# Turning one of six groups of probability blocks by a DMA transpose, in an attention and mixture-of-experts kernel on one NeuronCore

## The chip, the core and the metric

The kernel runs on one NeuronCore of a Trainium2 chip (trn2). The core has TensorE (PE in the profile; PEld are its weight loads), VectorE (DVE), ScalarE (ACT), GpSimd (POOL) and SyncE (SP, which here only issues DMAs). Every engine works through its own queue in order, and the engines wait for each other by semaphores. The metric is the time of one execution on the device, in microseconds (us); the median of several runs counts.

## The reference

The program computes block-causal attention over 8 batches of 8 heads, with 576 positions of 64 features, and then sends every position through one of 8 experts.

```python
scores = scale * np.matmul(q, k.transpose(0, 1, 3, 2))        # q, k, v: (8, 8, 576, 64)
mask = block_i >= block_j                                     # blocks of 64 positions
scores = np.where(mask, scores, -1000000000.0)
attn = softmax(scores); attn_out = np.matmul(attn, v)
x = attn_out.transpose(0, 2, 1, 3).reshape(B * S, H * D)      # 4608 x 512
expert_idx = np.argmax(x @ w_gate, axis=1)                    # one of 8, gate_w its probability
out[mask_e] = gate_w * (relu(x @ w1[e]) @ w2[e])              # w1: 512 x 1024, w2: 1024 x 512
```

All tensors are fp32.

## The kernel before, in words

The attention part works on 32 pairs of heads (four pairs to a batch). For one pair the queries are cut into four row blocks of 128 (`i` = 1 to 4) and a first block of 64; the two heads of the pair are `j` = 0 and 1, "A" and "B" in the names of the steps. The steps of a pair, with the lines that the profile shows:

- `ld` (L106 to L108) issues three DMAs on SP: keys `kd`, queries `qd`, values `v`, about 1 MB together. `cK`, `cQ` (ACT) and `lK`, `lQ` (DVE) split keys and queries into a high and a low part, so that scores come out of three products.
- `S1` to `S4`, `S0` (PE, L203 and L191) are the scores. The two heads run side by side on 64 rows of the array each. `K` (DVE memsets, L215) hides masked blocks, `M` (DVE, L220) takes the negative maximum of a row, `E` (ACT, L235) the exponential with its row sums. They write the probabilities `pb`, one fp32 tile of 128 partitions for a pair.
- The probabilities must be turned before they meet the values. That is done in six groups of four 128x128 blocks, `k0`, `a1`, `b1`, `a2`, `b2`, `x3`, and a small one, `t0`. `T` (PE, L274) transposes a group into a PSUM tile `pt` (two buffers), `H` (L286) copies it to an SBUF tile `ph` on the engine behind the `@` of its name.
- `V0` to `V5` (PE, L305) are the products with the values, the two heads on 64 columns of the array each. `V1` reads `a1` and `b1`, `V2` and `V4` read `a2` and `b2`, `V3` reads `x3`, `V0` reads `k0`, `V5` reads `t0`. `O`, `O0` copy the product out of PSUM.
- `F` (PE, L340 and L334) turns it back and multiplies by the gate's weights, `X`, `Y` (DVE) scale it. `R1`, `R2` (DVE) invert the sums, `Z` and `q0` (POOL) scale the small first block.

The order of all steps is written out by hand in the string `ORDER`. An entry `Tb1:3` means: in turn number t do step `Tb1` for pair t - 3. A turn goes through the whole string once, so each engine's queue gets its steps in that order, and four or five pairs are in work at a time. `z0` to `z6` are places for the router's small steps (one batch's after its fourth pair), `y0`, `y1` for pieces of POOL's work: scatters of the router's table and the splitting of the first expert's weights. When a batch is done, its rows go to memory by DMAs on SP (`xd`), about 1.1 MB.

The expert part follows when the last pair is done. It has a DMA transpose of its own, on ACT's queue (L996): ACT writes the two 16-bit halves of fp32 numbers as separate planes (L984), the DMA turns them, ACT joins them (L1002). The change does not touch that part.

Of the kernel before, what the change touches and what calls it, by code (L numbers as in the profile page):

```python
# [8 lines left out]
F32 = mybir.dt.float32  # L9
F32R = mybir.dt.float32r  # L10
BF16 = mybir.dt.bfloat16
U16 = mybir.dt.uint16
# [6 lines left out]
P = 128  # L19
# [11 lines left out]
POFF = (None, 0, 384, 1024, 1920)  # L31
PCOLS = 3072
# [7 lines left out]
class Attention:  # L40
# [8 lines left out]
    def __init__(self, ctx, tc, ident, qT, kT, vt, w_gate, ends, po):  # L49
# [8 lines left out]
        self.raw = ctx.enter_context(tc.tile_pool(name="araw", bufs=3))  # L58
        self.rawk = ctx.enter_context(tc.tile_pool(name="arawk", bufs=2))
        self.rawv = ctx.enter_context(tc.tile_pool(name="arawv", bufs=5))  # L60
        self.spl = ctx.enter_context(tc.tile_pool(name="aspl", bufs=2))
        self.pt = ctx.enter_context(tc.tile_pool(name="apt", bufs=9))
        self.sm = ctx.enter_context(tc.tile_pool(name="asm", bufs=3))
# [8 lines left out]
        self.bank, self.ptile, self.ph, self.oT, self.xs = {}, {}, {}, {}, {}  # L72
        self.small_bank, self.at = (None, None), {}
# [176 lines left out]
    def op_T(self, m, x):  # L250

# [5 lines left out]
        pb = self.pb[m]  # L260
        todo = {
# [6 lines left out]
        }.get(x)  # L268
# [4 lines left out]
        for n, o in enumerate(todo):  # L273
            self.nc.tensor.transpose(t[:, P * n : P * n + P], pb[:, o : o + P], self.ident)  # L274

    def copy(self, engine):
        return self.nc.scalar.copy if engine == "A" else self.nc.vector.tensor_copy
# [86 lines left out]
    def step(self, name, m):  # L364
# [9 lines left out]
        elif k == "T":  # L374
            self.op_T(m, name[1:])
# [19 lines left out]
    def run(self, order, sink, part, other, then, loaded):  # L395
# [9 lines left out]
        first = dict(order)["E1B"]  # L405
# [5 lines left out]
        for turn in range(self.M + last):  # L411
            if turn == first and dict(order)["S0"] < first:

                turns = [x for x in order if x[0] not in ("M0", "E0")]
                n = turns.index(("E1B", turn)) + 1
                turns[n:n] = [(x, turn) for x in ("S0", "M0", "E0")]
            else:
                turns = [x for x in order if x[0] != "S0" or turn > x[1] or x[1] == first]
            if turn == self.M + last - 1:
                turns = [(x, lag) for name, lag in order for x in ends.get(name, (name,))]  # L420
            for name, lag in turns:
# [11 lines left out]
                if not 0 <= m < self.M or (name == "ld" and m < 2):  # L433
                    continue
                self.step(name, m)
                if name == "ld":
                    loaded(m)
# [22 lines left out]
M1A:3 ld:0 V1:4 V3:4 V4:4 M1B:3 M3B:3 E1A:3 E1B:3 V5:4 Ta1:3 S0:3 lQ:2 E3B:3 z5:0 M0:3 z3:0 S4:2 O@A:4 Tk0:3 O0@D:4  # L460
z6:0 Ha1@A:3 Tb2:3 K4B:2 E0:3 q0:2 Hk0@A:3 F1:4 K4A:2 Hb2@A:3 M4B:2 M4A:2 X1:4 Tb1:3 E4B:2 y0:0 Y1:4 z4:0 z1:0 E4A:2
# [930 lines left out]
```

## Time and profile before

| | before |
|---|---|
| median of 3 runs | 830.76 us (830.45 to 830.93) |
| the profiled execution | 832.52 us |
| its span, from the first to the last instruction | 830.8 us |
| mean granted TensorE clock | 0.992 of full speed |
| PE, PEld, DVE, ACT, POOL busy | 808.1, 634.0, 420.8, 554.8, 357.0 us |
| HBM read, written | 76.76 MB, 21.98 MB |

A row of the profile names the line of the kernel, the engine, the operation and its tiles (out<-in, buffer numbers sometimes kept: `pt2b` is group b of pair 2), their shapes, and the time. Matmuls overlap each other, so the time from one start to the next says what one costs. The span is shorter than the execution's own time, 832.52 us, which holds what lies around the first and the last instruction.

### The profile page before, as it was taken

The numbers are of one execution on the slowest core, as the hardware profiler recorded it, in microseconds if no ns is written. First come the engines' busy times: TensorE is split into PE (matmuls) and PEld (weight loads), VectorE is DVE, ScalarE is ACT, GpSimd is POOL, SyncE is SP. The second block draws the span as 40 slices with busy tenths as digits, with TensorE's granted clock in tenths as the row PEclk, the third lists the DMA queues.
The fourth block names the chain that finished last, engine by engine and source line by source line (L and its number), as shares of the span: only waits on it lengthen the run. The fifth ranks groups of instructions, "written<-read, shape, count | busy, mean of one in ns | idle before, by whom it ended". The sixth has DMA issues, their size and how long they took to land.

```text
span 830.8 us, 16466 instructions
## 1 busy us (share of the span) xinstructions
PE 808.1 (97%) x5126; PEld 634.0 (76%) x5126; DVE 420.8 (51%) x1208; ACT 554.8 (67%) x1254; POOL 357.0 (43%) x392
## 2 busy tenths in 40 slices
PE   5999999999999999989899999999999999999996
PEld 4777777777777777768788888888888888888884
DVE  5677788888878878657604400046646444000000
ACT  6999899889898889724454555455546554554552
POOL 3000133333322502263745654466656655544553
PEclk8999999999999999999999999999999999999999
DMA  6335757464545537335826513346766853133212
GB/s 206 99 104 153 152 139 169 123 159 123 148 121 140 126 111 185 83 71 161 266 77 164 178 51 77 77 137 169 240 182 175 265 152 75 42 76 77 67 48 67
DMA packets 83706, 108.80 MB, mean 131 GB/s; under 512 B 45601, under 2 KB 48929, under 8 KB 83618
## 3 DMA queue, kind: packets, MB, share of 16 engines
q1 hardware_dynamic: 38082, 78.26, 33.1%
q0 software_dynamic: 7520, 19.97, 8.3%
q10 hardware_dynamic: 38016, 9.44, 6.8%
q8 instruction: 50, 0.82, 0.4%
q14 instruction: 38, 0.31, 0.1%
HBM read 76.76 MB, written 21.98 MB: 119 GB/s over the span
## 4 chain that ended last, share of the span: by engine, by line
PE 87%; issue 3%; POOL 2%; ACT 2%; DMA 1%; DVE 1%; POOLq 1%; DVEq 0%; SPq 0%; ACTq 0%
PE py L1058 23%; PE o L305 12%; PE ph L937 12%; PE o L937 12%; PE ya L203 6%; PE xa L203 3%; PE o L340 3%; PE px L896 2%; PE pt L1019 2%; PE o L334 1%; ACT pb L235 1%; POOL tab L732 1%; PE o L191 1%; DMA out<-y,idx 0%; PE o L1359 0%
## 5 line engine op out<-in xcount | busy, mean ns | idle before, releaser
L1058 PE MATMUL py<-w,low 128*128 (+1 forms) x912 | 226.9, 398 | 0.8 <-ACT low L1010 0.8
L1058 PEld LDWEIGHTS py<-w,low 128*128 128x128 f32 x912 | 168.8, 188 | 38.1 <-issue 1.2
L1181 DVE CAST w<-raw 128x1024 fp32r<-128x1024 f32 x60 | 49.3, 866 | 182.1 <-PE o L937 131.5
L248 POOL TENSOR_SCALAR p<-p,rs 128x64 f32<-128x64 f32 x32 | 14.2, 445 | 249.7 <-DVE rs L244 166.8
L1038 POOL TENSOR_TENSOR low<-h,low 128x512 fp32r<-128x512 f32 x72 | 105.2, 1464 | 24.7 <-ACT h L1011 24.7
L915 POOL TENSOR_TENSOR xl<-xf,xh 128x512 fp32r<-128x512 f32 x38 | 50.7, 1335 | 109.0 <-ACT xf L909 108.8
L1187 DVE TENSOR_TENSOR w<-raw,w 128x1024 fp32r<-128x1024 f32 x60 | 83.9, 1455 | 0.0
L906 ACT CAST xh<-px 128x512 fp32r<-128x512 f32 x38 | 22.3, 588 | 90.7 <-PE px L896 89.0
L937 PE MATMUL ph<-w,xh 128*128 x280 | 76.3, 395 | 0.0
L937 PE MATMUL o<-w,xh 128*128 x280 | 75.8, 393 | 0.0
L984 ACT COPY h<-ph 128x1024 uint16<-128x1024 uint16 x36 | 36.5, 1012 | 47.2 <-PE ph L937 26.0
L975 ACT ACTIVATE h<-o 128x512 f32<-128x512 f32 x37 | 22.2, 600 | 62.5 <-PE o L937 48.1
L937 PEld LDWEIGHTS ph<-w,xh 128*128 128x128 f32 x280 | 53.2, 190 | 12.1
L937 PEld LDWEIGHTS o<-w,xh 128*128 128x128 f32 x280 | 52.6, 188 | 11.7
L1082 POOL DMA_INDIRECT out<-y,idx x35 | 39.8, 1138 | 41.0 <-issue 37.0
L235 ACT ACTIVATE pb<-ya,neg 128x320 f32<-128x320 f32 (+2 forms) x93 | 48.6, 532 | 2.3 <-PE pt30x L274 1.6
L878 POOL DMA_INDIRECT xg<-xd,idx x37 | 45.3, 1226 | 10.2 <-POOL idx L874 9.2
L235 ACT ACTIVATE pb<-yb,neg 128x320 f32<-128x320 f32 (+2 forms) x93 | 49.4, 546 | 0.0
L732 POOL DMA_INDIRECT tab<-toks,posi x40 | 41.7, 1044 | 15.0 <-issue 14.2
L1002 ACT COPY h<-hf 128x1024 uint16<-128x1024 uint16 x36 | 43.3, 1203 | 5.1 <-DMA hf<-h 5.1
L220 DVE TENSOR_REDUCE neg<-ya 128x1 f32<-128x320 f32 (+2 forms) x93 | 44.8, 481 | 0.0
L220 DVE TENSOR_REDUCE neg<-yb 128x1 f32<-128x320 f32 (+2 forms) x93 | 41.9, 478 | 3.3 <-ACT pb L235 1.3
(966 smaller groups left out, 2132.3 us busy)
## 6 DMA issues: line engine op xcount, KB each, us to landing
raw<-w SPq DMA_DIRECT2D x60, 512.0 KB
qd<-qT SPq DMA_DIRECT2D x32, 352.0 KB
v<-vt SPq DMA_DIRECT2D x32, 352.0 KB
kd<-kT SPq DMA_DIRECT2D x32, 288.0 KB
xd<-xt SPq DMA_DIRECT2D x7, 1026.0 KB
xd<-xg SPq DMA_DIRECT2D x9, 256.5 KB
xg<-w SPq DMA_DIRECT2D x8, 256.0 KB
xd<-x SPq DMA_DIRECT2D x8, 128.0 KB
```

Of the source, the lines that this page charges most:

```text
L203: ins = mm(out, q[x][r, 128 * (i - 1) : 128 * i], q[y][r, o : o + w], start=n == 0, stop=n == 2, skip_group_check=True,)
L220: ins = self.nc.vector.tensor_reduce(self.neg[m][:, c : c + 1], src, AX.XY if i == 4 else AX.X, ALU.max, negate=True)
L235: ins = self.nc.scalar.activation(dst, src, AF.Exp, bias=self.neg[m][:, c : c + 1], scale=1.0, accum_out=self.sums[m][:, c : c + 1])
L305: self.nc.tensor.matmul(out[r], self.raws[m][2][:, slot], self.ph[m, bank][:, c0:c1], start=t in (0, 5), stop=t in (4, 5), skip_group_chec ...
L732: put = self.nc.gpsimd.indirect_dma_start(out=self.tab[:, :], out_offset=bass.IndirectOffsetOnAxis(ap=posi[:, i : i + 1], axis=0), in_=sel ...
L878: pool.indirect_dma_start(out=self.xg[i], out_offset=None, in_=self.xd[:, :], in_offset=bass.IndirectOffsetOnAxis(ap=self.idx[:, t : t + 1 ...
L915: pool.tensor_sub(self.xl, self.xf, self.xh).then_inc(sem["xp"], 1)
L937: m = pe.matmul(self.ph[f], x[:, P * k : P * k + P], weights(k, f, part), start=start and k == 0, stop=stop and k == 3,)
L1038: engine.tensor_sub(hl, self.hf if t < 2 else self.h[f], hh).then_inc(sem["hp"], 1)
L1058: m = pe.matmul(self.py[t % 2], h[:, c // 4, P * (c % 4) : P * (c % 4) + P], wf[:, bass.ds(off + (base + 512 * c), 512)], start=n == 0, st ...
L1181: dve.tensor_copy(hi, raw[m % nr]).then_inc(sem["wh"], 1)
L1187: dve.tensor_sub(lo, raw[m % nr], hi).then_inc(sem["wd"], 1)
```

## The change

The group `b1` is no longer transposed by PE. Three new steps take its place. `Db1` copies the four blocks to a tile of 16-bit numbers, first the low halves of all fp32 numbers, then the high halves (two buffers, which are halves of a weight buffer that is not yet in use, `raw[4]`). `Ib1` issues a DMA transpose of that tile on SP's queue. `Jb1` joins the two turned planes to fp32 numbers in a `ph` tile. The engines stand behind the `@` in the new order: `Db1@A` is on ACT, `Jb1@P` on POOL. For `Db1` to read the four blocks with one step, the places of the row blocks in `pb` move (`POFF`, and the tile grows from 3072 to 3840 columns).

The order of all steps is new. Two copies move from ACT to DVE (`Hb2`, `O`). `V1` and `V3` now come a turn later than `V0`, `V2`, `V4` and `V5` of the same pair. `qd` has four buffers instead of three, `kd` three instead of two, and the special places of `S0`, `M0`, `E0` in the first turns are worked out anew.

```diff
--- before.py
+++ after.py
@@ -28,8 +28,8 @@
 HIDE = -(2.0**100)
 
 
-POFF = (None, 0, 384, 1024, 1920)
-PCOLS = 3072
+POFF = (None, 0, 896, 1792, 2688)
+PCOLS = 3840
 VS = 11
 
 QS = 512 + P + D
@@ -46,7 +46,7 @@
 
 
 
-    def __init__(self, ctx, tc, ident, qT, kT, vt, w_gate, ends, po):
+    def __init__(self, ctx, tc, ident, qT, kT, vt, w_gate, ends, po, spare):
         self.tc, self.nc = tc, tc.nc
         self.qT, self.kT, self.vt = qT, kT, vt
         self.po = po
@@ -55,11 +55,12 @@
         self.M = qT.shape[0] * H // 2
         nc = self.nc
         cp = ctx.enter_context(tc.tile_pool(name="acst", bufs=1))
-        self.raw = ctx.enter_context(tc.tile_pool(name="araw", bufs=3))
-        self.rawk = ctx.enter_context(tc.tile_pool(name="arawk", bufs=2))
+        self.raw = ctx.enter_context(tc.tile_pool(name="araw", bufs=4))
+        self.rawk = ctx.enter_context(tc.tile_pool(name="arawk", bufs=3))
         self.rawv = ctx.enter_context(tc.tile_pool(name="arawv", bufs=5))
         self.spl = ctx.enter_context(tc.tile_pool(name="aspl", bufs=2))
         self.pt = ctx.enter_context(tc.tile_pool(name="apt", bufs=9))
+        self.pl = ctx.enter_context(tc.tile_pool(name="apl", bufs=2))
         self.sm = ctx.enter_context(tc.tile_pool(name="asm", bufs=3))
         self.ot = ctx.enter_context(tc.tile_pool(name="aot", bufs=2))
         self.xp = ctx.enter_context(tc.tile_pool(name="axp", bufs=2))
@@ -70,6 +71,8 @@
         self.raws, self.qs = {}, {}
         self.pb, self.sums, self.neg, self.rs = {}, {}, {}, {}
         self.bank, self.ptile, self.ph, self.oT, self.xs = {}, {}, {}, {}, {}
+        self.planes, self.turned = {}, {}
+        self.pl0 = [spare[:, 512 * i : 512 * i + 512].bitcast(U16) for i in range(2)]
         self.small_bank, self.at = (None, None), {}
         self.used = {}
         self.op_ld(0)
@@ -247,34 +250,56 @@
         t = self.p0[m]
         self.nc.gpsimd.tensor_scalar(t, t, self.rs[m][:, 8:9], None, ALU.mult)
 
-    def op_T(self, m, x):
-
-
-
-
+    def blocks(self, x):
 
         def at(j, i, t):
 
             return POFF[i] + (P * i + P * t if j else P * (i - t))
 
-        pb = self.pb[m]
-        todo = {
+        return {
             "k0": [POFF[i] + P * i for i in range(1, 5)],
             "a1": [at(0, i, 1) for i in range(1, 5)],
             "b1": [at(1, i, 1) for i in range(1, 5)],
             "a2": [at(0, 2, 2), at(0, 3, 2), at(0, 4, 2), at(0, 4, 4)],
             "b2": [at(1, 2, 2), at(1, 3, 2), at(1, 4, 2), at(1, 4, 4)],
             "x3": [at(0, 3, 3), at(0, 4, 3), at(1, 3, 3), at(1, 4, 3)],
-        }.get(x)
+        }[x]
+
+    def op_T(self, m, x):
+
         t = self.ptile[m, x] = self.ps_t.tile([P, 512], F32, tag="pt", name=f"pt{m}{x}")
         if x == "t0":
             self.nc.tensor.transpose(t[0:64, 0:P], self.p0[m], self.ident)
             return
-        for n, o in enumerate(todo):
-            self.nc.tensor.transpose(t[:, P * n : P * n + P], pb[:, o : o + P], self.ident)
+        for n, o in enumerate(self.blocks(x)):
+            self.nc.tensor.transpose(t[:, P * n : P * n + P], self.pb[m][:, o : o + P], self.ident)
+
+    def op_D(self, m, x, engine):
+
+        o = self.blocks(x)
+        assert all(b - a == o[1] - o[0] for a, b in zip(o, o[1:]))
+        step = 2 * (o[1] - o[0])
+        t = self.planes[m, x] = self.pl0[m % 2]
+        src = self.pb[m].bitcast(U16)[:, 2 * o[0] : 2 * o[0] + 3 * step + 256]
+        pad = self.pb[m].bitcast(U16)[:, 2 * o[0] : 2 * o[0] + 1]
+        src = bass.AP(pad.tensor, pad.offset, [list(pad.ap[0]), [1, 2], [step, 4], [2, P]])
+        self.copy(engine)(t.rearrange("p (o n c) -> p o n c", o=2, n=4), src)
+
+    def op_I(self, m, x):
+
+        t = self.turned[m, x] = self.pl.tile([P, 1024], U16, tag="tt", name=f"tt{m}{x}")
+        self.nc.sync.dma_start_transpose(t.rearrange("p (k c) -> p k c", c=P), self.planes.pop((m, x)))
+
+    def op_J(self, m, x, engine):
+
+        h = self.ph[m, x] = self.pt.tile([P, 512], F32, tag="ph", name=f"ph{m}{x}")
+        self.copy(engine)(
+            h.bitcast(U16).rearrange("p (c o) -> p o c", o=2),
+            self.turned.pop((m, x)).rearrange("p (o c) -> p o c", o=2),
+        )
 
     def copy(self, engine):
-        return self.nc.scalar.copy if engine == "A" else self.nc.vector.tensor_copy
+        return {"A": self.nc.scalar.copy, "D": self.nc.vector.tensor_copy, "P": self.nc.gpsimd.tensor_copy}[engine]
 
     def op_H(self, m, x, engine):
         t = self.ptile.pop((m, x))
@@ -371,8 +396,10 @@
             getattr(self, "op_" + name)(m, engine)
         elif k == "H":
             self.op_H(m, name[1:], engine)
-        elif k == "T":
-            self.op_T(m, name[1:])
+        elif k in "TI":
+            getattr(self, "op_" + k)(m, name[1:])
+        elif k in "DJ":
+            getattr(self, "op_" + k)(m, name[1:], engine)
         elif k == "Y":
             self.op_Y(m, int(name[1]), engine)
         elif k in "KME":
@@ -402,20 +429,16 @@
         last = max(lag for name, lag in order if name[0] not in "yz")
         left = [20] * (self.M // 4)
         more, pace, asks = iter(()), 1, None
-        first = dict(order)["E1B"]
+        at = {name: (lag, n) for n, (name, lag) in enumerate(order)}
+        after = max(("E1B", "E2B"), key=at.get)
+        late = ("S0", "M0", "E0") if at["S0"] < at[after] else ()
 
         ends = {
             "F1": ("F2", "F0"), "X1": ("X2", "Y0@D"), "Y1": ("Y2",), "F2": ("F1",), "X2": ("X1",), "Y2": ("Y1",),
             "F0": (), "Y0@D": (),
         }
         for turn in range(self.M + last):
-            if turn == first and dict(order)["S0"] < first:
-
-                turns = [x for x in order if x[0] not in ("M0", "E0")]
-                n = turns.index(("E1B", turn)) + 1
-                turns[n:n] = [(x, turn) for x in ("S0", "M0", "E0")]
-            else:
-                turns = [x for x in order if x[0] != "S0" or turn > x[1] or x[1] == first]
+            turns = order
             if turn == self.M + last - 1:
                 turns = [(x, lag) for name, lag in order for x in ends.get(name, (name,))]
             for name, lag in turns:
@@ -432,7 +455,12 @@
                     next(then)
                 if not 0 <= m < self.M or (name == "ld" and m < 2):
                     continue
+                if m == 0 and name in late:
+                    continue
                 self.step(name, m)
+                if m == 0 and name == after:
+                    for x in late:
+                        self.step(x, 0)
                 if name == "ld":
                     loaded(m)
                 if name == "F1" and asks == "bank":
@@ -457,10 +485,10 @@
 
 
 ORDER = """
-M1A:3 ld:0 V1:4 V3:4 V4:4 M1B:3 M3B:3 E1A:3 E1B:3 V5:4 Ta1:3 S0:3 lQ:2 E3B:3 z5:0 M0:3 z3:0 S4:2 O@A:4 Tk0:3 O0@D:4
-z6:0 Ha1@A:3 Tb2:3 K4B:2 E0:3 q0:2 Hk0@A:3 F1:4 K4A:2 Hb2@A:3 M4B:2 M4A:2 X1:4 Tb1:3 E4B:2 y0:0 Y1:4 z4:0 z1:0 E4A:2
-Ta2:3 z0:0 F0:4 F2:4 Hb1@A:3 cQ:1 S2:2 Ha2@A:3 R1:3 S1:2 lK:1 R2:3 X2:4 Y0@D:4 K1A:2 K2A:2 K2B:2 S3:2 M2A:2 Z:3 K1B:2
-K3A:2 Tx3:3 M2B:2 y1:0 cK:0 E2A:2 Hx3@A:3 M3A:2 K3B:2 Tt0:3 E2B:2 E3A:2 Ht0@D:3 z2:0 V0:3 V2:3 Y2:4
+Hx3@A:4 cK:1 Db1@A:3 y0:0 S4:2 V1:4 M0:3 Hb2@D:3 z4:0 Ib1:3 V3:4 Tk0:3 K4A:2 K4B:2 Ta1:3 M4A:2 E0:3 M4B:2 O@D:4 ld:0
+z3:0 E4A:2 E4B:2 F1:4 R1:3 lK:1 Y1:4 S1:2 S2:2 z1:0 z6:0 R2:3 X1:4 Hk0@A:3 S3:2 Ha1@A:3 F0:4 cQ:1 K1B:2 F2:4 z5:0
+M1B:2 Z:3 Ta2:3 q0:2 E1B:2 Ha2@A:3 K3B:2 K1A:2 M3B:2 Tt0:3 V0:3 K2A:2 K2B:2 V2:3 M2A:2 M1A:2 M2B:2 X2:4 z2:0 V4:3
+Y0@D:4 Y2:4 E3B:2 E2A:2 Ht0@D:3 V5:3 Jb1@P:3 Tx3:3 S0:2 K3A:2 M3A:2 E2B:2 lQ:1 E1A:2 Tb2:2 E3A:2 z0:0 O0@D:3 y1:0
 """
 
 
@@ -1286,7 +1314,7 @@
     po = ctx.enter_context(tc.tile_pool(name="pso", bufs=1, space=PSUM))
 
     with ExitStack() as actx:
-        att = Attention(actx, tc, ident, qT, kT, vt, w_gate, y, po)
+        att = Attention(actx, tc, ident, qT, kT, vt, w_gate, y, po, raw[4])
         router = Router(rcst, tp, sp, tc, B, xd, tab, ident)
 
         def weights(n):
```

## Rows read from the trace of the kernel before

**Rows 1.** The page: span, busy times, and the busy tenths of the span's 40 slices (20.8 us each) for DVE; PEclk is the granted TensorE clock in tenths of full speed.
```profile
span 830.8 us, 16466 instructions
...
PE 808.1 (97%) x5126; PEld 634.0 (76%) x5126; DVE 420.8 (51%) x1208; ACT 554.8 (67%) x1254; POOL 357.0 (43%) x392
...
DVE  5677788888878878657604400046646444000000
...
PEclk8999999999999999999999999999999999999999
```

**Rows 2.** Busy time by stretches of the attention part: from and to (us), length, busy us of PE, PEld, DVE, ACT and POOL with the number of instructions, granted clock, DMA share, GB/s. The first is a turn without the router's steps, the second the fullest of four turns in a row with them (203.10 to 245.80 us), the third the sum and the means of those four.
```profile
31.90:42.50 10.60, 10.60 (x95) 7.84 (x95) 7.87 (x29) 9.57 (x28) 0.94 (x3) 1.00 0.31 97
...
235.00:245.80 10.80, 10.71 (x95) 7.88 (x95) 9.23 (x35) 9.82 (x29) 2.87 (x5) 1.00 0.30 100
sum 42.70, PE 42.61 PEld 31.49 DVE 34.38 ACT 38.44 POOL 12.88; mean PE 10.65 PEld 7.87 DVE 8.60 ACT 9.61 POOL 3.22
```

**Rows 3.** Waits between 100 and 300 us, all engines: who waited for whom, us in total, times, longest.
```profile
DVE neg L220 <- PE o L191: 14.5, 18, 1.0
DVE xb L215 <- PE xb L203: 9.6, 14, 0.8
```

**Rows 4.** One turn of PE (pair 2 in most steps) in order of time: start us, us, what. L274 are the transposes `T`, L203 the scores `S`, L191 `S0`, L340 `F1` and `F2`, L271 `Tt0`, L305 the products `V`.
```profile
37.68 0.33 PE L191 MATMUL o<-qd,q 128*128 128x64 f32 x2
37.95 0.40 PE L203 MATMUL xa<-kh,qh 64*128 64x288 f32 x1
...
38.18 0.29 PE L203 MATMUL xa<-kl,qh 64*128 64x288 f32 x1
...
38.72 0.29 PE L203 MATMUL xa<-kh,ql 64*128 64x288 f32 x1
...
38.94 0.66 PE L274 MATMUL pt2k<-ident,pb 128*128 128x128 f32 x4
39.44 0.60 PE L274 MATMUL pt2b<-ident,pb 128*128 128x128 f32 x4
39.87 0.66 PE L340 MATMUL o<-fold,oT 128*128 128x144 f32 x4
40.37 0.60 PE L274 MATMUL pt2b<-ident,pb 128*128 128x128 f32 x4
40.80 0.62 PE L274 MATMUL pt2a<-ident,pb 128*128 128x128 f32 x4
...
44.30 0.27 PE L271 MATMUL pt2t<-ident,p 128*64 128x128 f32 x1
44.50 1.08 PE L305 MATMUL o<-ph2k,v 128*64 128x512 f32 x4
45.41 0.49 PE L305 MATMUL o<-ph2a,v 128*64 128x384 f32 x1
...
46.06 0.59 PE L305 MATMUL o<-ph2a,v 128*64 128x512 f32 x1
...
46.91 0.60 PE L305 MATMUL o<-ph2x,v 128*64 128x256 f32 x4
```

**Rows 5.** ACT: two steps of the same turn in order of time (a copy `H` and the exponential behind it), then the lines of the experts' own DMA transpose (planes, issue, join: count, duration min/median/max in ns) and the time from its issue to its landing.
```profile
40.12 0.59 ACT L286 COPY ph2b<-pt2b 128x512 f32<-128x512 f32 x1
40.60 0.76 ACT L235 ACTIVATE pb<-xb,neg 128x576 f32<-128x576 f32 x1
...
L984 ACT COPY h<-ph x36: 1012/1012/1016, 384.5 to 808.3; 128x1024 uint16<-128x1024 uint16 x36
L996 ACTq DMA_TRANSPOSE hf<-h x36: 1248/1252/2350, 386.8 to 809.4; - x36
L1002 ACT COPY h<-hf x36: 1163/1207/1212, 395.0 to 816.2; 128x1024 uint16<-128x1024 uint16 x36
...
DMA to landing us min/median/max: 3.9/4.1/8.1
```

**Rows 6.** DVE's copies from PSUM: count, duration min/median/max in ns, first and last start.
```profile
L316 DVE COPY o<-o x32: 211/214/241, 27.6 to 356.6; 128x64 f32<-128x64 f32 x32
L356 DVE COPY x<-o x32: 286/290/291, 32.1 to 358.5; 64x144 f32<-64x144 f32 x32
```

**Rows 7.** POOL's steps with one input (L248, L132) and with two (L1308), in the same form, and DVE's `lQ` (L123), whose longest is the one that starts at 282.47.
```profile
L248 POOL TENSOR_SCALAR p<-p,rs x32: 442/445/447, 19.9 to 352.5; 128x64 f32<-128x64 f32 x32
L132 POOL TENSOR_SCALAR q<-qd x32: 522/532/978, 5.4 to 334.1; 128x128 f32<-128x128 f32 x32
L1308 POOL TENSOR_TENSOR high<-xg,zero x8: 1266/1276/1290, 119.7 to 282.1; 128x512 fp32r<-128x512 f32 x8
L123 DVE SCALAR_TENSOR_TENSOR ql<-qd,qh x32: 671/681/1402, 5.3 to 336.6; 128x512 fp32r<-128x512 f32 x32
...
282.47 1.40 DVE L123 SCALAR_TENSOR_TENSOR ql<-qd,qh 128x512 fp32r<-128x512 f32 x1
```

**Rows 8.** ACT at the end of the attention part, in order of time: the last pair's last exponential and its row sum, and the copy of its product.
```profile
347.91 0.66 ACT L235 ACTIVATE pb<-yb,neg 128x448 f32<-128x448 f32 x1
348.43 0.24 ACT L235 ACTIVATION_READ_ACCUMULATOR pb<-yb,neg 128x1 f32 x1
...
356.47 0.59 ACT L312 COPY oT<-o 128x512 f32<-128x512 f32 x1 [2.70 <-PE o L305]
```

**Rows 9.** Busy time by stretches again, columns as in rows 2: ten microseconds in which a batch's rows are written.
```profile
222.00:232.00 10.00, 10.00 (x88) 7.26 (x88) 7.66 (x34) 9.17 (x27) 3.07 (x4) 1.00 0.99 201
```

## The prediction

> **What bounds the kernel now.** I read the page first, then a table of busy time by stretches, the waits, and one turn instruction by instruction. The page [rows 1] shows TensorE (PE) busy 97% of the span; the VectorE (DVE) digits end their dense part near the 18th of 40 slices of 20.8 us, which is where the 32 pairs of heads end (about 356 us); behind it come the experts, which the change does not touch. The granted clock there is full speed, 2.4 GHz, but for one early slice, so no term below is a clock term. The table [rows 2] is the view that decides: in a turn (one step of every kind, each for its own pair) PE is busy all of 10.60 us, ScalarE (ACT) 9.57, DVE 7.87, GpSimd (POOL) 0.94. Over four turns with the router's steps among them the means are 10.65 for PE, 9.61, 8.60 and 3.22, and the fullest turn has 9.23 of DVE. So PE sets the pace, ACT is 90% full, and DVE has some 2 us of slack a turn, partly spent waiting for PE itself, 14.5 and 9.6 us in 200 us on two lines [rows 3].
>
> A busy PE need not be at its peak, so the turn itself has to be read [rows 4]. Four 128x128 transposes cost 0.43 us where they follow their own kind (pt2b at 39.44 to 39.87, and 40.37 to 40.80). PE runs three tile shapes: 64-row scores (`64*128`), 64-column value products (`128*64`), and the full array. Where the shape changes, time is lost: the last scores at 38.72 to Tk0 at 38.94 is 0.22 against 0.135 inside the block (38.18 to 38.72 in four steps), and Tk0 then takes 0.50, not 0.43: together 0.15. From Tt0 (44.30) to V0 (44.50) is 0.20 against 0.11, and V0 takes 0.91 against 0.85 for the equal V1 (46.06 to 46.91): 0.15. S0 at 37.68 to the first scores and on to the second (37.95, 38.18) loses 0.25. The old order has six such changes a turn.
>
> **The change, part by part.** *Removed from PE:* Tb1, four transposes, 0.43 to 0.44 us a pair [rows 4]. That lies wholly on the engine that sets the pace.
>
> *Added to PE:* the new order puts V1 and V3 behind S4, apart from V0, V2, V4, V5. Counting along the order string, the shapes go scores, value, full, scores, full, value, full: seven changes where six stood. The new kind, scores to value, is not in the trace; it lies between 0 and the largest seen, 0.25, and I take 0.15, which both kinds nearest to it cost [rows 4]. The Trainium skill, TensorEngine Tiling (Array Packing), section Key Properties, says that changing the tiling mode drains the engine; the gaps at the changes of shape agree with it. By it the split has a price and the sum below stands at -3.9 us; without it the sum would be -8.6 (31 times 0.15 better). So PE's turn changes by -0.44 + 0.15 = -0.29 us, bounds -0.44 and -0.19.
>
> *ACT:* it loses three 128x512 copies (Hb1 goes, Hb2 and O move to DVE), 0.48 each from start to start (40.12 to 40.60, [rows 5]), and gains the planes Db1. The diff's order line has `Db1@A`: ACT makes the planes, and only the join is POOL's. The nearest rows are the experts' splits of as many 16-bit elements, 1.01 and 1.21 us [rows 5]; I take 1.1. Net -0.34: ACT goes to about 9.25 of 10.4 and does not set the pace.
>
> *DVE:* Hb2 and O, two copies of 128x512 from PSUM. DVE copies of 64 and 144 columns take 0.214 and 0.290 [rows 6]: 0.95 ns a column, so 0.64 for 512, about 0.6 from start to start; lower bound 0.5 (what ACT needs), upper 0.65. DVE gains 1.2 a turn: 9.8 mean, 10.43 in the fullest turn. Against PE turns of 10.36 mean and 10.51 for that fullest one, the slack that hid DVE's waits falls from 2.05 to 0.56 us. And the order leans on DVE: V5 on PE needs Ht0, which stands behind ten memsets and reductions, X2, Y0 and Y2 on DVE; F1 needs O, behind the four steps K4 and M4. DVE must wait for PE at least twice a turn, some 0.2 us each (scores to memset). So the fullest turn wants 10.43 + 0.4 = 10.83, 0.32 over PE; the others fit. That is 0.08 a turn on average; I take 0.10, bounds 0 and 0.5.
>
> *POOL:* the join Jb1, 1024 elements. Its one-input rows give 445 ns for 64 columns and 532 for 128 [rows 7]: 1.36 ns each, so 1.75 us; a two-input row, 1.28 for 512, gives 1.86 ns each, so 2.25. POOL rises from 3.2 to 5 us a turn and stays slack. Behind Jb1 on POOL stand one or two router or weight pieces, then q0 and Z half a turn later; S0 and Tt0 wait for those. A join late by under 3 us delays neither.
>
> *The transpose.* Ib1 stands on SP's queue before the next pair's loads and waits for Db1; behind it wait the loads, the batch's writes and the first expert's pieces. The loads are used a turn later, and they no longer wait for buffers (four and three instead of three and two), so an Ib1 in time costs them nothing. Landing took 4.1 us median, 3.9 to 8.1 [rows 5]. The chain, from the end of Tx3: Hx3, cK, Db1 on ACT 0.5 + 0.6 + 1.1 = 2.2 (cK has 576 columns, so a little over the copy's 0.48), up to 0.7 more for the exponential E3A that stands before Hx3 (one of its width took 0.66, [rows 8]), landing 4.1, join 1.75, semaphores 0.2: 8.9 us. V1 of that pair comes a turn and S0, Tb2, S4 later on PE (0.27 + 0.44 + 0.99, rows 4), at 12.1. So the whole chain is hidden, with 3.2 us to spare. After each batch SP's queue is full for 10 us (DMA share 0.99 from 222 to 232, [rows 9]); the writes are issued behind Ib1 of their turn, so the next Ib1 meets at most the last microsecond or two. I take 0.
>
> *Ends.* Startup has the same lags: 0, within 1 us. At the end nothing hides the chain. Before, the last exponential ends at 348.67 and the copy of the finished product starts at 356.47: 7.8 us [rows 8]. After: Hx3 0.5, planes 1.1, landing 4.1, join 1.75, V1 0.85 and V3 0.43 (half the columns), changes and semaphores 0.8: 9.6. I take +2 us, bounds 1 and 6 (landing 8.1).
>
> *Sum.* A turn: -0.44 + 0.15 + 0.10 = -0.19; 31 turns lie between the first pair and the last, so -5.9; ends +2.0; together -3.9 us. The profiled execution took 832.52 (span 830.8), so 828.6 for its like; it lies 1.8 above the median 830.76, for which I say 826.9.
>
> **Rivals.** *All hidden:* no price for the seventh change of shape, no wait for DVE: 31 times -0.44, ends +1.5, is -12 us, 818.6. For it: PE hardly waited before [rows 3]. Against it: the gaps at changes of shape.
>
> *DVE sets the pace (the other side):* place V5 behind Ht0, price DVE's total plus its waits. If 0.9 of the former 2.05 us of idle time stays, a turn is 9.8 + 0.9 = 10.7, 0.05 over the old mean; 31 turns and the ends give +3.6, 834.3. It decides from 0.23 us of PE waiting a turn, where the gain is gone. For it: the 10.43 of the fullest turn. Against it: the new order fills the two long waits of [rows 3] with the moved copies.
>
> *The join is late:* if landings under the pairs' loads are like the slowest row, 8.1, the chain needs 12.9 and V1 waits 0.8 us. In every second turn with a join at the upper bound (1.3 us) that is 16 times 1.3 = +21, with the other terms 844. For it: the loads share SP's queue; against it: the median 4.1 was taken under weight loads too.
>
> *POOL holds DVE up:* at 282.47 DVE's `ql` took 1402 ns instead of 681, under two POOL instructions [rows 7]. If the join met such a DVE step every turn, DVE would have 9.8 + 0.72 + 0.4 = 10.9 against PE's 10.36, 0.46 more than the forecast's 10.46: 31 times 0.46 is +14, 841. The join falls by my placing between lK and lQ, so only a late one meets them. The Trainium skill, SBUF — State Buffer, calls the port pair that both engines use an exclusive lock which blocks the loser for the whole instruction, for DVE steps with two SBUF inputs; the doubled row agrees.
>
> **Chances.** Forecast 0.42 (822 to 830), all hidden 0.20 (817 to 822), DVE 0.20 (831 to 837), late join 0.10 (837 and more), lock 0.08 (834 to 845). The range 818 to 838 leaves out the far ends of the first and the last two, about 0.17; the forecast's own is 822 to 830. This measurement tells some 0.2%, 1.7 us, from no change: faster (under 829.1) 0.58, same 0.12, slower 0.30.
>
> **What would show it.** PE's turn without router steps at 10.25 to 10.4 (10.60 now); a gap of 0.05 to 0.1 between S4 and V1; DVE 9 to 9.8 us in a turn; V5 with short waits on the copy of Ht0, none at V1; landings of 4 to 5 us; the join at 1.7 to 2.3. Long waits before V1, or joins that start late, prove the sum wrong; so does a DVE that never idles beside a PE that does.

## The result: 0.9% slower, and the profile after

The changed kernel took 838.64 us (median of 3 runs, 837.36 to 838.91) where the kernel before took 830.76: a ratio of 1.0091, 95% interval 1.0068 to 1.0114. The forecast was 826.9 with a range to 838, so it was wrong in sign and just outside its range. The page after, in the rows that answer to [rows 1]:

```profile
span 836.4 us, 16259 instructions
...
PE 807.2 (97%) x4998; PEld 615.6 (74%) x4998; DVE 465.9 (56%) x1272; ACT 539.1 (64%) x1190; POOL 397.7 (48%) x424
```

PE is still 97% busy: its sum says nothing of what happened. The table by stretches, as in [rows 2], does: a turn without router steps, then the turns of pairs 10, 14 and 18.

```profile
41.05:51.58 10.53, 10.48 (x91) 7.27 (x91) 9.13 (x31) 9.06 (x27) 2.22 (x3) 1.00 0.41 121
104.70:118.33 13.63, 12.57 (x103) 8.32 (x101) 10.91 (x40) 9.34 (x27) 4.97 (x8) 1.00 1.11 168
151.50:164.10 12.60, 12.56 (x103) 8.32 (x101) 10.93 (x40) 9.34 (x27) 4.97 (x8) 1.00 1.00 163
196.30:208.96 12.66, 11.93 (x104) 8.16 (x100) 11.74 (x39) 9.35 (x28) 5.04 (x8) 1.00 0.77 155
```

The turn without router steps went from 10.58 to 10.53, and once in every four turns stands one of 11.75 to 13.6 us, where before none exceeded 11.4. DVE is 10.9 to 11.7 us busy in those. From the rounding of q of pair 2 to that of pair 31 it is 319.6 us (310.9 before). The last copy oT of the attention part starts 9.2 us later; the experts' start then takes 3.6 us less, so that 5.6 remain in the span. The waits from 100 to 300 us, as in [rows 3]:

```profile
PEld o L330 <- DVE h L308: 7.6, 6, 1.6
PE o L330 <- DVE h L308: 6.2, 5, 1.3
PE o L330 <- POOL ph8b L296: 1.0, 1, 1.0
POOL ph8b L296 <- DMA tt8b<-raw: 6.5, 1, 6.5
POOL ph12b L296 <- DMA tt12b<-raw: 5.5, 1, 5.5
```

Two new waits: V5 for the copy Ht0 (6.2 us of PE; the 7.6 us of its weight loads, PEld, are the same waits seen a second time), and the join for transposes issued behind a batch's writes, with V1 behind it. These landed late: tt8b 10.1 us after issue, where the next one took 3.6.

```profile
tt8b<-raw SPq DMA_TRANSPOSE x1, 10.1
tt9b<-raw SPq DMA_TRANSPOSE x1, 3.6
```

V1 has two halves, one for each head, which start together in other turns. For pair 8 the half that reads b1 starts 2.09 us after the half that reads a1, as soon as the join ends:

```profile
111.65 1.07 PE L330 MATMUL o<-ph8a,v 128*64 128x512 f32 x2
113.74 0.64 PE L330 MATMUL o<-ph8b,v 128*64 128x512 f32 x1 [1.02 <-POOL ph8b L296]
```

### The profile page after: what moved, and what is told of

Its sections match the earlier page's. It is cut to its first block, busy times and chain, and to the rows that moved or that the text cites. A ratio compares the mean times of both kernels' runs of the same rounds, so it can differ in the third digit from the quotient of the medians.

```text
span 836.4 us, 16259 instructions
## 1 busy us (share of the span) xinstructions
PE 807.2 (97%) x4998; PEld 615.6 (74%) x4998; DVE 465.9 (56%) x1272; ACT 539.1 (64%) x1190; POOL 397.7 (48%) x424
## 4 chain that ended last, share of the span: by engine, by line
PE 80%; DVE 9%; ACT 3%; DMA 3%; issue 2%; POOL 2%; POOLq 0%; SPq 0%; DVEq 0%; ACTq 0%
PE py L1086 24%; PE ph L965 12%; PE o L965 12%; PE o L330 7%; DVE neg L223 4%; PE ya L206 4%; PE o L365 4%; PE xa L206 3%; PE px L924 2%; PE pt L1047 2%; ACT pb L238 2%; DMA tt8b<-raw 1%; PE o L359 1%; DMA tab<-toks,posi 1%; DVE oh L656 1%
## 5 line engine op out<-in xcount | busy, mean ns | idle before, releaser
L1066 POOL TENSOR_TENSOR low<-h,low 128x512 fp32r<-128x512 f32 x72 | 107.8, 1500 | 22.1 <-ACT h L1039 22.1
L965 PEld LDWEIGHTS ph<-w,xh 128*128 128x128 f32 x280 | 52.6, 188 | 11.9
L238 ACT ACTIVATE pb<-yb,neg 128x192 f32<-128x192 f32 (+2 forms) x93 | 49.4, 531 | 18.5 <-DVE neg L223 18.5
L1110 POOL DMA_INDIRECT out<-y,idx x35 | 37.5, 1071 | 40.9 <-issue 36.6
L906 POOL DMA_INDIRECT xg<-xd,idx x37 | 44.7, 1208 | 10.4 <-POOL idx L902 10.4
L365 PE MATMUL o<-fold,oT 128*128 128x144 f32 x256 | 44.3, 296 | 2.2 <-DVE m L643 0.9
L223 DVE TENSOR_REDUCE neg<-yb 128x1 f32<-128x192 f32 (+2 forms) x93 | 45.2, 486 | 0.4
## 6 DMA issues: line engine op xcount, KB each, us to landing
xd<-xt SPq DMA_DIRECT2D x7, 1026.0 KB, 12.7
```

The lines of the kernel that those rows point to most:

```text
L223: ins = self.nc.vector.tensor_reduce(self.neg[m][:, c : c + 1], src, AX.XY if i == 4 else AX.X, ALU.max, negate=True)
L238: ins = self.nc.scalar.activation(dst, src, AF.Exp, bias=self.neg[m][:, c : c + 1], scale=1.0, accum_out=self.sums[m][:, c : c + 1])
L365: mm(t[:, i], self.oT[m, 0][:, o : o + P], w, start=True, stop=True)
L906: pool.indirect_dma_start(out=self.xg[i], out_offset=None, in_=self.xd[:, :], in_offset=bass.IndirectOffsetOnAxis(ap=self.idx[:, t : t + 1 ...
L965: m = pe.matmul(self.ph[f], x[:, P * k : P * k + P], weights(k, f, part), start=start and k == 0, stop=stop and k == 3,)
L1066: engine.tensor_sub(hl, self.hf if t < 2 else self.h[f], hh).then_inc(sem["hp"], 1)
```

## The experiments

Eighteen runs: the first eight take the change apart, the others its long turns and what is left. Ratios are to the kernel before in the same session.

**The order and the transpose apart.** The new order with b1 back on PE:

```diff
-... Db1@A:3 ... Ib1:3 ... Jb1@P:3 ...
+... Tb1:3 Hb1@A:3 (where the join stood) ...
```

> The changed kernel in its new order, but b1 is transposed by PE again (Tb1 and its copy Hb1 on ACT stand where the join stood; planes, DMA transpose and join are gone). PE has 0.44 us more a turn: about 14 us if PE sets the pace. Queue theory: the losses of the batch turns (about 10 us) go with the DMA transpose, so 838.6 + 14 - 10 = 842. DVE theory: the batch turns keep their length and only the quiet turns grow, 848 to 850.

881.0 us, 1.0587 (1.0563 to 1.0610), far above both expectations: in the new order the transpose by DMA is worth 42 us against `Tb1` and `Hb1` at that place, the only one that was tried. A turn without router steps takes 12.15 us there, 1.6 more, for 0.44 of PE's work. The old order with the DMA transpose, planes on POOL:

```diff
-... E3B:3 z5:0 ... X1:4 Tb1:3 E4B:2 ... F2:4 Hb1@A:3 cQ:1 ... M2B:2 y1:0 ...
+... E3B:3 Db1@P:3 Ib1:3 z5:0 ... X1:4 E4B:2 ... F2:4 cQ:1 ... M2B:2 Jb1@P:3 y1:0 ...
```

> b1 goes by the DMA transpose as in the changed kernel, but in the old order, with the copies Hb2 and O on ACT as before, and with the planes made by POOL: Db1 and Ib1 stand behind E3B, the join before y1. PE loses 0.44 us a turn and no change of shape is added, ACT loses 0.48, DVE keeps 8.6, POOL gains 2.7. If the new order with its DVE copies is what costs (order theory), 818 to 826 us. If the DMA transpose itself costs (its landing, POOL's join beside DVE), 832 to 850.

847.95 us, 1.0178 (1.0132 to 1.0224). Its turn without router steps, in the columns of [rows 2]:

```profile
49.40:59.97 10.57, 10.23 (x89) 7.42 (x87) 7.87 (x28) 9.02 (x26) 3.64 (x6) 1.00 0.53 147
```

PE is busy 0.37 us less, the turn is as long as before, and DVE is as busy as before (its total is lost in turns of 11.5 to 15.5 us, in the longest of which POOL holds planes and join up). The chain of work in that turn shows why:

```profile
49.49 0.03 issue
...
49.81 1.24 DVE neg L223 x2
51.05 0.06 issue
51.11 0.42 DVE xt L374
...
51.77 0.48 PE o L359 x2
```

The last scores S4 release M4 on DVE, behind which X1 stands, and F0 on PE follows X1. From the last product of S4 to F0 it takes 2.59 us in both kernels, before with Tb1 in between (38.72 in [rows 4] to 41.31), here with a wait of 0.34:

```profile
41.31 0.48 PE L334 MATMUL o<-fold,o 128*128 128x144 f32 x2
...
49.18 0.29 PE L206 MATMUL xa<-kh,ql 64*128 64x288 f32 x1
...
51.77 0.48 PE L359 MATMUL o<-fold,o 128*128 128x144 f32 x2 [0.34 <-DVE rs L244]
```

The turn is a loop through PE and DVE, and Tb1 had stood in a stretch that the loop leaves free. With the planes on ACT (`Db1@A` in that order) it is longer:

> The same in the old order, but the planes are made by ACT: ACT gains 0.55 us a turn instead and stands at 10.1 of 10.2. Order theory: a little behind old_order_pool, 822 to 832 us. If the transpose itself costs: 832 to 850.

(`Db1@A:3` in place of `Db1@P:3`.) 854.14 us, 1.0296 (1.0232 to 1.0361), above both expectations; the turn 10.88. Then I tried to shorten the loop by the order, with and without the transpose:

```diff
-... Ha1@A:3 Tb2:3 K4B:2 ... Hk0@A:3 F1:4 ... M4B:2 M4A:2 X1:4 ... Y1:4 ...
+... Ha1@A:3 F1:4 K4B:2 ... Hk0@A:3 Tb2:3 ... M4B:2 X1:4 Y1:4 M4A:2 ...
```

> The old order with b1 turned by the DMA and planes and join on POOL (847.95, its turn without router work 10.57 us, as long as before although PE has 0.44 us less to do), with three moves: F1 on PE goes ahead of Tb2, and X1 and Y1 on DVE go ahead of M4A and E4B's place. Theory (the old turn is a loop that leaves PE through S4, runs over DVE's M4 and X1 and comes back at F0, so that PE's saved 0.44 us is spent as a wait at F0): with X1 and Y1 earlier that wait goes and the turn without router work falls to about 10.15 to 10.3 us. Rival (something else, ACT or the scores themselves, holds the turn): it stays at 10.5 to 10.6.

> The kernel before, b1 on PE as it was, with the same three moves as the run beside it (F1 ahead of Tb2; X1 and Y1 ahead of M4A). Theory (PE's own work of 10.5 us is as long as the loop over DVE, so nothing can be gained until Tb1 is gone): the same time within 2 us of 830.8, turn without router work 10.5 to 10.6. Rival (F0's wait for DVE was part of the old turn too): 3 to 8 us faster.

860.98 (1.0355, 1.0319 to 1.0392) and 858.08 (1.0330, 1.0284 to 1.0376), with turns of 11.38 and 11.43: both expectations failed. Three moves lengthen the turn by 0.8 us; which of them does was not told apart, so that the loop rests on the chains shown and was not shortened by any run.

**The moved copies.** Hb2 and O back on ACT, O alone back on ACT, and the kernel before with both on DVE:

```diff
-... Hb2@D:3 ... O@D:4 ...
+... Hb2@A:3 ... O@A:4 ...
```

> The changed kernel, but the copies Hb2 and O are back on ACT. DVE theory: DVE falls by 1.2 us a turn, the batch turns of 12 to 13.6 us fall to about 11, F1's wait for O shortens: 825 to 830 us. Queue theory: the late landings stay, 836 to 839. Third possibility: ACT, then at about 10 of 10.5 us, takes DVE's place: 838 to 845.

> The changed kernel with the copy O alone back on ACT (0.6 us less on DVE a turn, 0.48 more on ACT). If DVE is the pace in the batch turns and F1 waits for O on DVE in all: 828 to 834. If the order balances both engines so that either way loses: 840 to 850, between the changed kernel and copies_act (858.9).

> The kernel before, in its old order and with all transposes on PE, with one edit: the copies Hb2 and O on DVE. DVE theory: DVE at 9.8 of 10.65 us starts to hold PE, 834 to 838 us. Queue theory: no change, 830 to 832.

858.94 (1.0311, 1.0286 to 1.0336), 858.94 (1.0314, 1.0275 to 1.0352), 871.32 (1.0462, 1.0440 to 1.0483). All three took longer than any of their expectations said. The turns without router steps are 11.05, 11.0 and 11.95. In the changed kernel the copies' place on DVE is worth 0.5 us a turn; in the old order the same move costs 1.4.

**The batch's writes.** Issued on ACT's queue, and in two halves a turn apart on SP's:

```diff
...
-            put.append(nc.sync.dma_start(self.by_partition(b, c0, c1), xt[:, :, c0:c1]))
+            put.append(nc.scalar.dma_start(self.by_partition(b, c0, c1), xt[:, :, c0:c1]))
```

```diff
...
-        self.rows(b, xt, x0, 0, RW)
+        self.rows(b, xt, x0, 0, RW, 0)
+        yield
+        self.rows(b, xt, x0, 0, RW, 1)
```

> The changed kernel, but a batch's rows (1.1 MB, once in four turns) are issued on ACT's DMA queue, so the transpose no longer queues behind them on SP's. Queue theory (the transpose lands 5 to 10 us after its issue once a batch, the join is late, V1 waits and DVE is held up): seven or eight batches lose 1.3 to 2 us less each, 825 to 830 us, and no transpose lands later than 5 us. DVE theory (DVE's two more copies set the pace in the turns with the router's steps): at most 3 us better, 835 to 839, with V5's waits on Ht0 as before.

> The changed kernel, but a batch's rows are written in two DMAs of half the size, one turn apart, so that SP's queue is never full for a whole turn; no engine has more to do. Queue theory: no transpose lands later than 5 us, the turns behind a batch lose their 1.1 us wait before V1, and the following turn some of its 2 us: 825 to 832 us. DVE theory: 835 to 839.

850.86 (1.0215, 1.0189 to 1.0241) and 844.47 (1.0163, 1.0116 to 1.0211), both above either expectation. With the writes on ACT's queue the transposes land 3.0 to 3.7 us after issue (the last pair's 6.2), but ACT stands still for 1.7 us around the issue of the larger write (91.51 to 93.19), and turns that had been 10.7 become 12.4. Halves leave the long turn at 12.1 even where the join starts 4.3 us after the transpose's issue, as early as elsewhere (the turns of pairs 18 and 22); V5 still waits 1.34 us for Ht0 behind each of them. So the landing is not the only price of that turn.

**DVE's place in the long turn.** Two of the seven places for router steps go to the end of the turn; or Ht0 goes ahead of X2:

```diff
-... F2:4 z5:0 ... X2:4 z2:0 V4:3 ... O0@D:3 y1:0
+... F2:4 ... X2:4 V4:3 ... O0@D:3 z5:0 z2:0 y1:0
```

> The changed kernel with two of its seven places for router steps moved: the place behind F2 and the one between X2 and V4 go to the end of the turn, behind O0. No instruction is added or taken away; only where DVE meets the router's work changes. Theory (the turns with router work are long because DVE's router steps stand ahead of X2, Y0, Y2 and the copy Ht0, for which the value product V5 on PE waits): V5's waits for Ht0, 13.8 us between 100 and 300 us, mostly go, the long turn of each batch falls from 12 to 13.6 us to about 11, and the time is 825 to 832. Rival (the place does not matter, DVE's total or the late landings do): 837 to 841, and the wait shows up at another instruction.

```diff
-... M2B:2 X2:4 z2:0 V4:3 ... Ht0@D:3 V5:3 ...
+... M2B:2 Ht0@D:3 X2:4 V4:3 ... V5:3 z2:0 ...
```

> The changed kernel with the DVE copy Ht0 moved ahead of X2, Y0 and Y2 (where the order before had it ahead of Y2), and the place for router steps that stood ahead of V4 moved behind V5. Theory (Ht0's place on DVE makes V5 wait): no wait of V5 for Ht0 is left beyond 3 us between 100 and 300 us; if those waits are the price of the long turns, 826 to 832. Rival (DVE is simply full in these turns, so that what is late moves on to X2, Y0 and F1): 836 to 841, with waits for DVE at F1, F0 or the scores instead.

840.1 (1.0109, 1.0076 to 1.0143) and 841.36 (1.0131, 1.0097 to 1.0165). Both take the waits for Ht0 away, and the total does not show it. The turns do. This table is worked out from the traces: turns of 4 pairs apart, from one rounding of q to the next, and the whole from pair 2 to 31.

| kernel | 6 | 10 | 14 | 18 | 22 | 26 | 30 | quiet | 2 to 31 |
|---|---|---|---|---|---|---|---|---|---|
| before | 10.8 | 11.0 | 11.1 | 10.8 | 10.8 | 11.2 | 10.8 | 10.58 | 310.9 |
| after | 12.0 | 13.6 | 12.6 | 12.7 | 12.0 | 12.7 | 11.8 | 10.53 | 319.6 |
| z_late | 11.0 | 13.4 | 13.6 | 11.0 | 11.9 | 12.7 | 11.0 | 10.55 | 316.2 |
| z_wpool | 11.0 | 11.0 | 11.0 | 11.0 | 11.0 | 12.7 | 11.0 | 10.54 | 310.2 |
| z_flush | 11.0 | 11.0 | 11.0 | 11.0 | 11.0 | 11.0 | 11.0 | 10.54 | 308.5 |

The rounding of q is a step of ACT, and a long turn can be made up in the next: in the changed kernel pair 6's turn of 12.0 is followed by one of 9.4, together 21.4 as before (21.3). By sums of four turns the changed kernel loses nothing from pair 6 to 9 (42.7, before 42.7) and from 26 to 29 (43.5, 43.7); it loses 3.9, 1.8, 2.2 and 1.4 us in the four batches from pair 10 to 25, those whose transposes landed late (10.1, 9.1, 7.2 and 6.6 us after issue).

In z_late the turns of pairs 6, 18 and 30 are short; those of 10, 14, 22 and 26 are not. The chain through the turn of pair 10 names what is left:

```profile
102.37 9.91 DMA tt8b<-raw
...
112.40 1.34 POOL ph8b L296
...
113.81 0.10 POOL L L633
...
113.93 0.20 DVE m L643
...
115.15 1.38 DVE neg L223 x2
116.53 0.60 DVE oT L337
...
117.28 0.73 PE o L365 x4
```

Two ways lead from the late join to PE. V1, which uses it, starts its second half late: from the last product of S4 to Tk0 PE takes 1.90 us more than the 1.66 of other turns (idle for 0.8 of it). The other is a detour, and in z_late it ends last: behind the late join POOL's queue holds the 0.10 us memset of the router's `L`, DVE's maximum over `L` waits for that, behind it stand M4 and the copy O, and F1 on PE waits another 0.96 us for O. In the changed kernel itself F1 does not wait in this turn; V1's 2.08 us are the price there, and 1.05 and 1.16 us for pairs 12 and 24.

**Landings and POOL's block.** On top of z_late: rows in halves; rows of the first six batches on POOL's queue; halves and two weight steps instead of one per place on POOL:

```diff
-put.append(nc.sync.dma_start(self.by_partition(b, c0, c1), xt[:, :, c0:c1]))
+q = nc.gpsimd if b < self.B - LATE else nc.sync
+...
+put.append(q.dma_start(self.by_partition(b, c0, c1), xt[:, :, c0:c1]))
```

```diff
             elif todo and here:
                 todo.pop(0)()
+                if todo and len(here) < 4:
+                    todo.pop(0)()
```

> The run with two router places moved to the end of the turn (840.1), and besides the rows of each batch written in two halves a turn apart. Theory (the two causes add: DVE's steps ahead of Ht0, and landings behind the writes): landings behind the batches fall to 2.6 to 7 us, the turns of pairs 10 and 14 fall from 13.4 and 13.6 to 11 to 12, and the last pair's scores begin 3 to 5 us earlier; time 834 to 838. Rival (the landings cost nothing, DVE's total is what is left): those turns stay above 13 and the time at 839 to 842.

> The run with two router places moved (840.1), and the rows of the first six batches issued on POOL's DMA queue instead of SP's. Theory (the transpose waits behind the batch's writes in its own queue): its landing falls to 2.6 to 3.2 us, the turns of pairs 10 and 14 fall from 13.4 and 13.6 to about 11, turn 26 stays at 12 to 12.7 because POOL's weight steps hold the join there, and the time is 832 to 837. Rival (the 16 DMA engines are shared, so another queue does not help): landings stay at 5 to 9 us and the time at 838 to 842.

> The run with two router places moved and the rows written in halves, and besides POOL takes two weight steps in a place instead of one in the first batches, so that fewer are left for the block of them that it works off at the sixth batch. Theory (in turn 26 the join stands behind that block on POOL): the join of that pair starts 4 to 6 us after its transpose is issued instead of 9 to 10, the turn falls from 12.6 to about 11, 1.5 us less than the run without it. Rival (the turn is long for DVE's sake): it stays at 12 or more.

837.0 (1.0053, 1.0023 to 1.0082), 833.02 (1.0004, 0.9983 to 1.0025) and 840.18 (1.0102, 1.0069 to 1.0135). With POOL's queue tt8b lands in 6.2 instead of 9.9 us (2.6 to 3.2 were expected) and the turns of pairs 10 and 14 are 10.97 and 10.96. Halves repair these two as well (10.97, 11.45), but make one of 14.9 us, where a DVE step X waits for the rows to leave the batch's buffer. Two weight steps at a time shorten the turn of pair 26 from 12.7 to 11.3 and lengthen three others to 12.1 to 12.6: beside these steps two router steps of DVE with five columns each take 1.24 and 1.21 us (the second has a median of 0.16 in the changed kernel).

**The block moved behind the join, and the last pair on PE.** The weight steps left at the sixth batch are done two to a place, after the join; then the last pair's b1 goes back to PE:

```diff
-                while todo:
-                    todo.pop(0)()
+                here.append(here[-1])
...
+                if todo and len(here) > B - LATE - 1:
+                    todo.pop(0)()
```

> The run with two router places moved and the batches' rows on POOL's queue (833.0), and besides the block of about four weight steps that POOL works off at the sixth batch, ahead of the join of pair 24, is spread over the next places of POOL, two steps in each, all behind that join. Theory (the join stands behind that block): the turn of pair 26 falls from 12.65 to about 11.0, the time to 830 to 832. Rival (these steps cost the same wherever they stand, by DVE's slower steps beside them): 832.5 to 834, the time lost in the next turns.

```diff
...
     def op_I(self, m, x):

+        if m == self.M - 1:
+            self.op_T(m, x)
+            self.op_H(m, x, "A")
+            return
...
```

> As the run beside it, and the last pair's b1 is turned on PE and copied on ACT, at the place where the transpose was issued, with no planes, transfer or join for that pair. Theory (at the end nothing hides the chain of planes, transfer and join, 2 us more than before): from the last exponential to the last oT it takes about 8 us instead of 9.9, and the time is 1.5 to 2.5 us below the run beside it. Rival (the drain is held by V4, V5 and the copies in any order): within 0.8 us of the run beside it.

830.63 (1.0016, 0.9996 to 1.0036) and 833.99 (1.0037, 1.0016 to 1.0058). The turn of pair 26 falls to 10.98, as expected. The drain, from the end of the last exponential's row sum to the last copy oT, is 7.8 us before, 9.7 after and in z_flush, and 10.5 with b1 on PE, where 2 us less were expected: it does not hang on the transpose. In z_flush the last join ends at 352.8 and V1 starts at 354.97.

```profile
351.46 1.35 POOL L296 COPY ph31b<-tt31b 128x1024 uint16<-128x1024 uint16 x1 [0.33 <-DMA tt31b<-raw]
...
354.97 0.64 PE L330 MATMUL o<-ph31a,v 128*64 128x512 f32 x1
```

**One change of shape fewer.** z_flush with V1 and V3 behind V5 of the same pair (the join, Ta2, Tx3 and Hx3 move with them; none was tried alone):

```diff
-Hx3@A:4 ... S4:2 V1:4 ... V3:4 Tk0:3 ... Ta2:3 ... V5:3 Jb1@P:3 Tx3:3 S0:2 ...
+... S4:2 ... Tk0:3 ... Ta2:3 F0:4 ... Tx3:3 q0:2 Jb1@P:3 E1B:2 Ha2@A:3 Hx3@A:3 ... V5:3 V1:3 V3:3 S0:2 ...
```

> As z_flush (830.6 beside a kernel before at 829.9), and V1 and V3 on PE stand right behind V5 of the same pair again, so that PE changes its tile shape six times a turn instead of seven; for that the join goes half a turn earlier on POOL, Ta2 ahead of F0, Tx3 ahead of Tt0 and its copy Hx3 behind Ha2. Theory (the seventh change costs PE 0.3 us a turn and PE sets these turns): the turn without router steps falls from 10.53 to 10.2 to 10.3 us, the drain by some 1.5 us, the time to 819 to 824, below the kernel before. Rival (DVE and ACT set the turn by now, or V1 waits for a join with less to spare): 10.5 us or more, 828 to 836.

871.81 us, 1.0487 (1.0458 to 1.0516), where the theory said 819 to 824. PE's busy time fell by 0.21 us (from the 10.48 of the changed kernel) and the turn grew by 1.2 us:

```profile
44.10:55.80 11.70, 10.27 (x91) 7.18 (x89) 9.22 (x32) 9.16 (x26) 2.23 (x3) 1.00 0.39 111
```

```profile
52.41 0.11 DVE xa L218
...
52.60 1.38 DVE neg L223 x2
53.98 0.60 DVE oT L337
...
54.73 0.73 PE o L365 x4
```

From S4 by M4 and O to F1, DVE takes 2.3 us, and PE waits 1.43 of them. In the changed kernel V1, V3, Tk0 and Ta1 fill that stretch of PE (47.92 to 50.45); here only Tk0 and Ta1 are left in it. The seventh change of shape is the price of a cover.

## Why the prediction was wrong

**Tb1 off PE, -0.44 a turn: this step failed.** I read "busy all of 10.60" in [rows 2] as "PE sets the pace", and so counted each microsecond of its work as one of the turn. In the old order the removal was worth nothing (old_order_pool), and in the changed kernel a turn without router steps fell to 10.53 us, by 0.05, where 10.25 to 10.4 was forecast. What sets the turn, by the chains of old_order_pool and six_changes, is a loop over S4, DVE's M4 and O or X1, and F1 or F0; busy PE work either lies on it or covers it.

**The seventh change, 0.15.** PE's busy time is 0.21 us lower in six_changes, with the same instructions; so the price was about 0.2, within the bound of 0.25, if no other change of shape fell into the idle time there. Beside it F1 waits for O: in the changed kernel O ends at 50.30 and F1 starts at 50.45 instead of at 50.28, after Ta1's 0.43 us: 0.17.

**Waits for DVE, 0.10 a turn: mis-sized.** I named the place, V5 behind Ht0, and priced DVE by its total against PE's: some 2 us between 100 and 300 us, where PE waited 6.2 us for Ht0, in five turns. In a loop not the total but the position counts: with the same DVE work, moving two router places removed these waits and took 3.4 us off the stretch from pair 2 to 31 (part of it came back as longer waits for the join, 2.06 instead of 1.05 us for pair 12). The rival "DVE sets the pace" had the right engine and place, and its 834.3 was too low by the same reading.

**The chain hidden, the next transpose meets "the last microsecond or two": this failed too.** The transposes tt8b, tt12b, tt16b and tt20b, behind batches, landed after 10.1, 9.1, 7.2 and 6.6 us, and the 3.2 us of spare time were used up: z_wpool, with the writes on another queue, takes 5.9 us off the stretch of z_late. The rival of the late join had the right victim, V1, at the wrong frequency: 2.08, 1.05 and 1.16 us in three turns, not 1.3 in 16 (its 844 would be 848 with the sum's own terms). I had listed a router piece behind the join on POOL, but followed only q0 and Z, not the router's `L` to DVE, which is the longer way in z_late. Nor had I asked what stands ahead of the join: a block of weight steps held that of pair 24 for 4.5 us after its landing, and moving the block is worth 1.7 us (z_flush).

**Right in size.** Planes 1.06 us (1.1), landing 3.2 median (4.1), DVE's copies 0.68 long and 0.60 from start to start (0.6). The join took 1.34, less than the 1.75 forecast (and its upper bound of 2.25 comes to 2.2 when worked out again from [rows 7]). ACT fell to 9.06 (9.25). DVE beside POOL: `ql` at 201.21 took 1.60 us instead of 0.68, with a join from 200.98 to 202.32. The Trainium skill, SBUF — State Buffer, section Who interferes with whom, says that a DVE instruction with two SBUF inputs contends with a GpSimd instruction that reads SBUF; this row agrees. Over the attention part such excesses sum to about 3.7 us (0.7 before), not all on the chain.

```profile
201.21 1.60 DVE L126 SCALAR_TENSOR_TENSOR ql<-qd,qh 128x512 fp32r<-128x512 f32 x1
...
200.98 1.34 POOL L296 COPY ph16b<-tt16b 128x1024 uint16<-128x1024 uint16 x1 [3.57 <-PE o L330]
```

**The drain, +2.0: right number, wrong cause.** It measured 1.9 (the terms of its sum make 9.5, not 9.6), but the join was ready 2.2 us before its use, and turning the last pair on PE made it longer: the number was luck. What holds the drain was not found.

**What stays open.** From the start of the last oT to that of the experts' 100th product into `py` it took 72.2 us before, 68.6 after, and 68.8 to 75.0 in the other kernels, all of which leave the experts as they are. The chain passes through different engines there; why was not tried. Even with all long turns repaired the time is that of the kernel before (830.63 against 829.93), and no run beat it: 2.3 us won between pairs 2 and 31, 1.9 lost in the drain. Of those 2.3 us 1.1 lie in the turn of pair 2 alone (9.46 for 10.56; 11.13 in z_flush_last, with the same order), so that the other 28 turns won 1.2, 0.04 each.

## What to carry to other kernels

An engine that is busy all the time does not set the pace if part of its work only fills the time in which another engine's step of the loop runs: before you price a removed instruction, follow the loop once round and look whether the instruction stands on it or covers it. When a step can be late, list what is queued behind it on its own engine and follow that to the end, small memsets too; the consumer of its result need not be the only one that pays. When a change shows several long turns, tabulate them turn by turn over the experiments, since causes that hide each other in the total fall one by one there, and look at the sums of neighbouring turns too, since a long one can be made up in the next.

## What the runs showed of the hardware

Behind 1.0 MB of writes on SP's queue the transpose tt8b landed after 9.9 us (z_late), with the writes on POOL's queue after 6.2 (z_wpool); the medians are 4.1 (of only eight landings that this trace shows) and 3.1 (of 25). The queue, and not the shared transfer engines alone, made it late. POOL's copy of 1024 elements of 16 bits took 1.34 us, a quarter less than the 1.75 that its 32-bit steps in [rows 7] give for as many. And a DVE step of five columns, with one input, was held for 1.2 us beside one of POOL's two-input steps in z_halves_spread, and ended 0.03 us after it: not the size of the DVE step but that of POOL's set the price.

```profile
134.35 1.21 DVE L744 TENSOR_SCALAR g<-g 128x5 f32<-128x5 f32 x1
...
134.25 1.28 POOL L1335 TENSOR_TENSOR low<-xg,high 128x512 fp32r<-128x512 f32 x1
```
